# Output turns in 64-row tiles, idle matmuls at the start, and a new order for a fused linear-attention and highway kernel

## The chip, the cores and the metric

The kernel runs on one core of a Trainium2 chip. A core has engines with streams of their own: TensorE (PE, matrix products, with its weight loads shown as PEld), VectorE (DVE), ScalarE (ACT), GpSimd (POOL) and the queues that issue transfers (mainly SyncE, SP). They wait for one another through semaphores. Operands lie in on-chip memory of 128 partitions (SBUF); results of TensorE go to PSUM[...]. The metric is device time of one execution in microseconds (us), lower being better.

## What is computed

Linear attention with a decay per head, in blocks of 64 positions, and behind it a highway layer over all tokens:

```python
# q, k, v: (4, 8, 768, 64); lam: (8,)
for b in range(nb):                          # blocks of 64
    intra = einsum('bhic,bhjc->bhij', qb, kb) * Dmask      # lam^(i-j), lower triangle
    intra = einsum('bhij,bhjd->bhid', intra, vb)
    inter = einsum('bhid,bhde->bhie', qb * lam_pow, kv_state)
    out[block] = intra + inter
    kv_state = lam_block * kv_state + einsum('bhsd,bhse->bhde', kb_dec, vb)

x = out as (3072, 512)                       # tokens x heads*dim
H = maximum(x @ w_h, 0)
T = sigmoid(x @ w_t + b_t)
return T * H + (1 - T) * x                   # float32
```

The kernel works in steps of 256 tokens: 12 steps, three for each of the 4 batch entries. Powers of lam are put into q and v when they are scaled, so that the mask is a plain triangle. The highway result is formed as x + T (H - x).

## The kernel before

Nothing is left to a scheduler: a long string, PLAN, lists operations in order, and each engine runs its own in that order. A token such as `TQ.3.2=0` names the operation, its step and part, and after `=` the PSUM banks; `@ACT` names an engine. What the tokens stand for:

- `Lk/Lq/Lv`: loads of half a step (256 KB, rows of 512 bytes). `W`: half of one weight matrix (512 KB). `CK/CQ/CV`: cast or scaling to bf16. `WC`: cast of weights.
- `TQ/TK`: transposes of q and k on TensorE; `EQ/EK`: their copies out of PSUM.
- `S`, `U`, `SS`: scores and state updates; `KE`: copy of the state; `M`: mask; `I`, `A`: the parts of the attention output from the state and from within the block; `D`: copy of it to bf16, as xT (features x tokens).
- `F.n.u.w`: two 128-feature rows of a product of the highway layer, w=0 for H and w=1 for T; `H`: relu and subtraction; `G`: sigmoid; `X`: th = T (H - x).
- `R`: the output turn, from features x tokens back to tokens x features; `E`: its copy to SBUF; `ST`: its store. `Z`: idle matmuls (the plan before has none).

```python
def trans(x, n, p, bk):                       # TQ, TK: 128x128 tiles
    ...
            T.transpose(t[:, i, j, :], get(x + "b", n)[:, j, h:h + 2, :], id128)

def score(n, e, hp, j, b):                    # 64x64 tiles of the array, 128 columns moved
    T.matmul(get("s", n, e, hp // 2)[half(b), hp % 2, j, :], lhsT=get("kT", n)[half(e), hp, j, half(b)],
             rhs=get("qT", n)[half(e), hp, :, half(b)], start=True, stop=True)

def intra(n, u):                              # A: 16 matmuls in 64x64 tiles
    for hp in (2 * u, 2 * u + 1):
        for j in range(J):
            for b in range(2):
                for e in range(2):
                    T.matmul(get("o", n, b)[half(e), hp, :], lhsT=get("vs", n)[half(b), 2 * hp + e, j, :],
                             rhs=get("m", n, e, u)[half(b), hp % 2, j, :], ...)

def block(i, u, w, bk):                       # F: 8 matmuls of 256 columns, 128x128 tiles
    g, z = group(i)
    t = bank(("ht"[w], g, u), bk[0], [128, 2, z * C])
    for r in range(2):
        for kc in range(KC):
            T.matmul(t[:, r, :], lhsT=w_b[w][:, kc, (2 * u + r) * 128:(2 * u + r + 1) * 128],
                     rhs=get("xT", *g)[:, kc, :], start=(kc == 0), stop=(kc == KC - 1))

def turn(n, b, p, bk):                        # R: 8 matmuls of 128 columns for 128 tokens, one bank
    ...
    for a, j in enumerate(js):
        for i, x in enumerate((get("xT", *g), get("th", g))):
            T.matmul(t[:, a * 128:(a + 1) * 128], lhsT=x[:, j, r * C:(r + 1) * C], rhs=id128,
                     start=(a == 0 and i == 0), stop=(i == 1), skip_group_check=True)

def store(n, b, p):                           # ST: 256 KB for 128 tokens
    i = (2 * n + b) * C
    nc.sync.dma_start(out=out[i:i + C, cs], in_=get("o_sb", n, b, p))

def load_w(w, g):                             # W: 256 columns, rows of 1 KB
    cs = slice(256 * g, 256 * g + 256)
    nc.sync.dma_start(out=w_f[w][:, :, cs], in_=(moe_w_h, moe_w_t)[w][:, cs].rearrange("(kc p) m -> p kc m", p=128))
```

A turn is a product with the identity that adds x and th in PSUM as it transposes them: per step two calls (b = 0, 1) of 8 matmuls each. The last step is split in groups of 128 tokens (and its second 128 tokens' output in two halves), to shorten the end.

Of the kernel before, what the change touches and what calls it, by code (L numbers as in the profile page):

```python
# [17 lines left out]
Lq.0.0 Lq.0.1 Lq.1.0 Lk.0.1 Lv.0.1 Lk.0.0 Lv.0.0 Lk.1.0 CQ.0.1@POOL Lq.1.1 Lv.1.1 CQ.0.0@POOL CK.0.1@ACT Lk.1.1  # L18
TQ.0.0=0 TQ.0.1=1 Lv.1.0 TK.0.1=2 EK.0.1@DVE CK.0.0@POOL Lq.2.1 CV.0.1@DVE TK.0.0=3 EQ.0.1@DVE CV.0.0@POOL Lk.2.0
EQ.0.0@DVE S.0.1=45 EK.0.0@DVE Lq.2.0 U.0.0 S.0.0=62 B=1 KE.0.0@DVE CQ.1.2@POOL W.0.1 M.0.1.0 U.0.1 M.0.0.1 Lk.2.1  # L20
M.0.0.0 CK.1.2@POOL TQ.1.2=0 KE.0.1@DVE I.0=32 W.0.0 EQ.1.2@ACT CV.1.2@POOL TK.1.2=4 M.0.1.1 Lv.2.0 EK.1.2@DVE A.0.1
A.0.0 D.0.1@ACT SS.1.1=60 Lv.2.1 CQ.2.2@POOL KE.1.0@ACT M.1.1.1 W.1.1 D.0.0@ACT M.1.1.0 SS.1.0=54 WC.0.1.0@ACT I.1=20
M.1.0.1 WC.0.1.1@POOL Lk.3.1 TQ.2.2=3 M.1.0.0 CK.2.2@POOL F.0.1.0=6 EQ.2.2@ACT W.1.0 BC A.1.0 WC.0.0.0@DVE
WC.0.0.1@POOL Lk.3.0 A.1.1 TK.2.2=4 D.1.1@ACT D.1.0@DVE F.0.0.0=5 EK.2.2@DVE Lq.3.1 F.1.1.0=1 CV.2.2@POOL KE.1.1@DVE
Lq.3.0 H.0.1 F.1.0.0=3 Lv.3.0 H.1.1 WC.1.1.0@ACT SS.2.0=02 WC.1.1.1@POOL H.0.0 Lv.3.1 SS.2.1=46 M.2.0.0 F.0.1.1=1
Lq.4.1 M.2.1.0 F.1.1.1=5 WC.1.0.1@ACT WC.1.0.0@POOL Lq.4.0 KE.2.0@DVE G.0.1@ACT F.0.0.1=0 M.2.1.1 CK.3.2@POOL Lv.4.1
G.1.1@ACT X.0.1@DVE F.1.0.1=4 Lk.4.0 G.0.0@ACT M.2.0.1 I.2=61 CQ.3.2@POOL Lk.4.1 X.1.1@DVE G.1.0@ACT A.2.0 A.2.1
X.0.0@DVE Lv.4.0 TK.3.2=2 D.2.1@ACT H.1.0 R.0.1.2=5 EK.3.2@ACT Lk.5.1 CV.3.2@POOL TQ.3.2=0 X.1.0@DVE R.0.0.2=1 Lq.5.0
EQ.3.2@ACT D.2.0@DVE R.1.1.2=3 R.1.0.2=4 Lk.5.0 E.0.1.2@ACT CQ.4.2@POOL SS.3.1=26 F.2.1.0=0 Lv.5.0 KE.3.0@ACT M.3.1.1
E.0.0.2@ACT Lv.5.1 M.3.1.0 SS.3.0=56 E.1.0.2@ACT TQ.4.2=1 CK.4.2@POOL Lq.5.1 M.3.0.1 KE.3.1@ACT F.2.1.1=2 EQ.4.2@ACT  # L30
H.2.1 Lq.6.0 CV.4.2@POOL TK.4.2=4 M.3.0.0 G.2.1@ACT I.3=60 Lq.6.1 F.2.0.0=1 EK.4.2@DVE X.2.1@DVE Lv.6.0 A.3.1
SS.4.1=54 H.2.0 CK.5.2@POOL Lq.7.0 A.3.0 F.2.0.1=2 KE.4.0@DVE D.3.1@ACT Lk.6.0 M.4.1.1 D.3.0@ACT SS.4.0=10 G.2.0@ACT
M.4.1.0 CV.5.2@POOL Lk.6.1 F.3.1.1=6 M.4.0.1 Lq.7.1 F.3.0.1=4 X.2.0@DVE Lv.6.1 KE.4.1@DVE CQ.5.2@POOL I.4=50 G.3.0@ACT
F.3.0.0=2 M.4.0.0 Lk.7.1 E.1.1.2@ACT TK.5.2=1 H.3.0 G.3.1@ACT ST.0.0.2 F.3.1.0=3 CQ.6.2@POOL X.3.0@DVE EK.5.2@ACT
Lk.8.1 TQ.5.2=2 H.3.1 R.2.0.2=4 EQ.5.2@ACT Lq.8.1 X.3.1@DVE R.2.1.2=1 A.4.0 E.2.0.2@DVE CK.6.2@POOL Lv.7.1 E.2.1.2@ACT
A.4.1 SS.5.1=36 D.4.1@DVE SS.5.0=24 Lk.7.0 CQ.7.2@POOL D.4.0@DVE R.3.1.2=1 Lv.7.0 TQ.6.2=0 M.5.1.0 E.3.1.2@ACT
TK.6.2=5 M.5.1.1 EQ.6.2@ACT ST.3.1.2 F.4.0.0=3 CV.6.2@POOL M.5.0.1 Lq.8.0 KE.5.0@ACT F.4.1.0=1 M.5.0.0 R.3.0.2=6
EK.6.2@DVE I.5=04 H.4.0 E.3.0.2@ACT SS.6.1=25 H.4.1 ST.3.0.2 A.5.0 A.5.1 ST.1.0.2 KE.6.0@DVE F.4.1.1=6 Lq.9.0
CK.7.2@POOL D.5.0@DVE Lk.9.0 SS.6.0=31 Lq.9.1 G.4.1@ACT D.5.1@DVE F.4.0.1=0 M.6.0.0 KE.6.1@ACT Lk.9.1 F.5.1.1=4
M.6.1.1 G.4.0@ACT Lk.8.0 CQ.8.2@POOL X.4.1@DVE F.5.0.1=3 G.5.1@ACT Lq.10.1 M.6.1.0 F.5.1.0=5 X.4.0@DVE Lv.8.0  # L40
CV.7.2@POOL TK.7.2=6 M.6.0.1 Lv.8.1 TQ.7.2=2 EK.7.2@DVE R.4.1.2=0 Lv.9.0 EQ.7.2@DVE F.5.0.0=1 E.4.1.2@ACT H.5.1
Lk.11.0 G.5.0@ACT I.6=62 A.6.0 H.5.0 SS.7.1=05 CK.9.2@POOL ST.0.1.2 A.6.1 X.5.0@DVE TQ.8.2=1 D.6.1@ACT Lv.9.1
X.5.1@DVE CK.8.2@POOL R.4.0.2=3 D.6.0@ACT TK.9.2=2 KE.7.0@DVE ST.2.1.2 R.5.0.2=4 CQ.9.2@POOL Lq.10.0 M.7.1.0
EK.9.2@ACT F.6.1.0=6 Lq.11.0 E.4.0.2@DVE E.5.0.2@ACT TK.8.2=0 M.7.1.1 EQ.8.2@ACT SS.7.0=23 CV.8.2@POOL H.6.1 ST.1.1.2
TQ.9.2=4 Lk.11.1 EK.8.2@ACT M.7.0.1 F.6.1.1=5 EQ.9.2@DVE I.7=16 Lq.11.1 G.6.1@ACT M.7.0.0 F.6.0.0=3 Lv.10.0
CV.9.2@POOL KE.7.1@ACT X.6.1@DVE SS.8.0=04 Lv.11.1 H.6.0 A.7.1 A.7.0 SS.8.1=25 Lk.10.0 D.7.0@DVE R.5.1.2=3
CQ.10.2@POOL D.7.1@DVE F.6.0.1=1 ST.5.0.2 M.8.0.0 F.7.1.0=6 Lk.10.1 G.6.0@ACT M.8.0.1 CK.11.2@POOL TQ.10.2=0 Lv.11.0
M.8.1.1 KE.8.0@ACT F.7.1.1=4 X.6.0@DVE EQ.10.2@ACT ST.2.0.2 CQ.11.2@POOL F.7.0.0=5 Lv.10.1 M.8.1.0 E.5.1.2@ACT H.7.1
R.6.0.2=1 G.7.1@ACT ST.4.0.2 H.7.0 I.8=02 ST.5.1.2 E.6.0.2@ACT A.8.1 X.7.1@DVE SS.9.1=36 A.8.0 F.7.0.1=5 KE.9.0@ACT
M.9.1.0 M.9.1.1 SS.9.0=14 G.7.0@ACT D.8.0@DVE TK.11.2=3 CK.10.2@POOL D.8.1@DVE KE.9.1@ACT TQ.11.2=6 R.6.1.2=0  # L50
EK.11.2@ACT X.7.0@DVE TK.10.2=2 M.9.0.0 CV.10.2@POOL F.8.1.0=5 E.6.1.2@ACT EK.10.2@DVE EQ.11.2@ACT ST.6.1.2 F.8.0.0=3
M.9.0.1 ST.6.0.2 ST.4.1.2 H.8.1 R.7.1.2=1 CV.11.2@POOL I.9=02 H.8.0 SS.10.1=64 E.7.1.2@ACT A.9.1 A.9.0 KE.10.0@ACT
M.10.1.1 SS.11.0=53 D.9.1@ACT SS.10.0=14 M.11.0.0 D.9.0@ACT F.8.1.1=2 M.10.0.0 R.7.0.2=5 M.10.0.1 I.10=01 M.10.1.0
E.7.0.2@ACT F.9.1.0=4 KE.10.1@DVE ST.7.0.2 A.10.0 ST.7.1.2 M.11.0.1 A.10.1 SS.11.1=56 D.10.1@ACT F.8.0.1=3 KE.11.0@DVE
G.8.1@ACT F.9.1.1=1 D.10.0@ACT X.8.1@DVE G.8.0@ACT F.9.0.1=0 H.9.1 G.9.1@ACT X.8.0@DVE F.10.1.0=2 M.11.1.0 G.9.0@ACT
F.10.0.0=4 M.11.1.1 R.8.0.2=3 X.9.1@DVE I.11=56 E.8.0.2@ACT A.11.0 A.11.1 ST.8.0.2 R.8.1.2=1 D.11.1@DVE F.10.1.1=3
E.8.1.2@ACT H.10.0 D.11.0@ACT F.9.0.0=6 H.10.1 G.10.1@ACT F.10.0.1=1 H.9.0 F.12.0.0=4 X.9.0@DVE G.10.0@ACT F.12.0.1=5
R.9.0.2=2 X.10.0@DVE F.11.1.1=6 E.9.0.2@ACT H.12.0 F.11.0.1=0 G.12.0@ACT X.10.1@DVE ST.9.0.2 F.11.1.0=1 ST.8.1.2
R.9.1.2=2 G.11.1@ACT X.12.0@DVE F.11.0.0=4 H.11.1 E.9.1.2@ACT R.10.1.2=3 H.11.0 G.11.0@ACT ST.9.1.2 R.10.0.2=5
X.11.1@DVE F.12.1.1=1 E.10.1.2@ACT X.11.0@DVE F.12.1.0=2 E.10.0.2@DVE ST.10.1.2 G.12.1@ACT R.11.1.0=4 R.11.0.2=6  # L60
H.12.1 ST.10.0.2 E.11.1.0@ACT X.12.1@DVE ST.11.1.0 E.11.0.2@ACT R.11.1.1=0 ST.11.0.2 E.11.1.1@DVE ST.11.1.1
"""

BUFS = dict(kf=5, qf=5, vf=5, kb=3, qb=2, vs=3, kT=2, qT=3, m=8, xT2=3, xT1=2, th2=2, th1=2, hm2=3, hm1=2, tb2=2, tb1=2, ss=4, o=10, oh=2)
# [3 lines left out]
def kernel(  # L68
# [13 lines left out]
    C = 128  # L82
# [30 lines left out]
    make_identity(nc, id128)  # L113
    tk_i = singles.tile([128, NST, J], I32)
# [10 lines left out]
    V.tensor_copy(id_f, id128[0:KC, 0:KC])  # L125
    ln_bc = singles.tile([128, H], F32)
# [8 lines left out]
    A.preload_act_table(AF.Sigmoid)  # L135
# [14 lines left out]
    def new(key, shape, dtype=BF16, tag=None):  # L150
        if key not in made:
            tag = tag or key[0]
            made[key] = sb.tile(shape, dtype, tag=tag, name=tag, bufs=BUFS[tag])
        return made[key]
# [15 lines left out]
    def load(x, n, p):  # L170
        b, c = divmod(n, NST)
        hs = heads(p)
        nc.sync.dma_start(out=new((x + "f", n), [128, H, J * D], F32)[:, hs],  # L173
                          in_=SRC[x][b, hs, c * 2 * C:(c + 1) * 2 * C, :].rearrange("h (p j) d -> p h (j d)", j=J))

    def load_w(w, g):
        cs = slice(256 * g, 256 * g + 256)
        nc.sync.dma_start(out=w_f[w][:, :, cs], in_=(moe_w_h, moe_w_t)[w][:, cs].rearrange("(kc p) m -> p kc m", p=128))

    def cast_w(w, g, i, eng):  # L180
        ks, cs = slice(2 * i, 2 * i + 2), slice(256 * g, 256 * g + 256)
        copy(eng, w_b[w][:, ks, cs], w_f[w][:, ks, cs])
# [161 lines left out]
    def spin(r, bk, idle=[0]):  # L344
        idle[0] += 1
        t = bank(("spin", idle[0]), bk[0], [128, 128])
        for _ in range(r):
            T.matmul(t, lhsT=id128, rhs=id128, start=True, stop=True)

    DO = {  # L350
        "Lk": lambda a, e, bk: load("k", *a), "Lq": lambda a, e, bk: load("q", *a), "Lv": lambda a, e, bk: load("v", *a),
# [8 lines left out]
        "X": lambda a, e, bk: gate(*a, e), "R": lambda a, e, bk: turn(*a, bk), "E": lambda a, e, bk: evac_o(*a, e),  # L360
# [38 lines left out]
```

## Time and profile before

| | before |
|---|---|
| time, median of 3 | 112.09 us (112.01 to 112.38) |
| span of the profiled execution | 109.5 us |
| PE / PEld busy | 95.4 / 84.8 us |
| DVE / ACT / POOL busy | 84.0 / 66.3 / 60.8 us |
| read / written | 20.98 / 6.29 MB |
| packets of the load and store queue, share of 16 engines | 86.0% |

Busy time of PE is a sum over overlapping, pipelined matmuls, so the start of one matmul to the start of the next tells more than its duration. In the groups by line, the columns are: line, engine, operation, output<-inputs, shapes and count, then busy us and mean ns of one, then the idle time ahead of it and what ended it. In the chain of work in order of time, a row has its start, its length, and the engine, output tile and line, with the number of instructions merged. `bx` is the output turn's PSUM tile, `bh`/`bt` those of the highway products, `bqtr`/`bktr` of the transposes, `bs` of scores, `bo` of the attention output, `kv` the state.

### The profile page before, as it was taken

The numbers are of one execution on the slowest core, as the hardware profiler recorded it, in microseconds if no ns is written. First come the engines' busy times: TensorE is split into PE (matmuls) and PEld (weight loads), VectorE is DVE, ScalarE is ACT, GpSimd is POOL, SyncE is SP. The second block draws the span as 40 slices with busy tenths as digits, with TensorE's granted clock in tenths as the row PEclk, the third lists the DMA queues.
The fourth block names the chain that finished last, engine by engine and source line by source line (L and its number), as shares of the span: only waits on it lengthen the run. The fifth ranks groups of instructions, "written<-read, shape, count | busy, mean of one in ns | idle before, by whom it ended". The sixth has DMA issues, their size and how long they took to land.

```text
span 109.5 us, 4558 instructions
## 1 busy us (share of the span) xinstructions
PE 95.4 (87%) x1969; PEld 84.8 (77%) x1969; DVE 84.0 (77%) x144; ACT 66.3 (61%) x120; POOL 60.8 (55%) x51
## 2 busy tenths in 40 slices
PE   0007887999999999999999999999999999999960
PEld 0005776878889888999888998889898888999950
DVE  0204794739996699799999899899999968867870
ACT  3581034453599867595528279709686639666970
POOL 6073797748489966969737679699319300000000
PEclk9999999999999999999999999999999999999998
DMA  0999999999999999999999999999955331020584
GB/s 9 268 294 291 290 292 328 321 322 317 282 270 299 299 291 297 291 293 301 315 355 313 291 297 314 360 340 310 343 193 195 111 128 70 0 96 6 192 301 178
DMA packets 43899, 27.55 MB, mean 252 GB/s; under 512 B 1764, under 2 KB 40936, under 8 KB 43880
## 3 DMA queue, kind: packets, MB, share of 16 engines
q1 hardware_dynamic: 43728, 27.27, 86.0%
q8 instruction: 15, 0.25, 1.0%
q14 instruction: 4, 0.03, 0.1%
q10 hardware_dynamic: 152, 0.01, 0.1%
HBM read 20.98 MB, written 6.29 MB: 249 GB/s over the span
## 4 chain that ended last, share of the span: by engine, by line
PE 80%; SPq 5%; DMA 5%; DVE 2%; POOL 2%; ACT 2%; issue 1%; DVEq 0%
PE bt L301 20%; PE bh L301 19%; PE bx L328 9%; PE bs L217 8%; PE bo L282 6%; PE bqtr L205 6%; SPq L173 5%; PE bktr L205 5%; DMA qf<-in_q_dram 5%; PE bo L272 5%; PE kv L222 2%; POOL qb L191 2%; DVE o L105 1%; ACT ss L103 1%; ACT o L103 1%
## 5 line engine op out<-in xcount | busy, mean ns | idle before, releaser
L301 PEld LDWEIGHTS <-w_b 128*128 128x128 bf16 x416 | 37.3, 99 | 4.9 <-issue 0.2
L256 DVE TENSOR_TENSOR m<-bs,tri 128x512 bf16<-128x512 f32 x48 | 31.0, 679 | 4.1 <-PE bs L217 3.9
L315 ACT ACTIVATE bt<-bt,bt_col 128x256 f32<-128x256 f32 (+1 forms) x52 | 22.0, 431 | 8.5 <-PE bt L301 5.6
L191 POOL TENSOR_TENSOR qb<-qf,pow_q 128x1024 bf16<-128x1024 f32 (+1 forms) x13 | 23.0, 1772 | 7.0 <-ACT pow_v L134 3.6
L301 PE MATMUL bh<-xT,w_b 128*128 128x256 bf16 (+1 forms) x208 | 25.1, 269 | 0.0
L191 POOL TENSOR_TENSOR vs<-vf,pow_v 128x1024 bf16<-128x1024 f32 (+1 forms) x12 | 22.0, 1835 | 5.5 <-DMA vf<-in_v_dram 5.5
L301 PE MATMUL bt<-xT,w_b 128*128 128x256 bf16 (+1 forms) x208 | 24.0, 265 | 0.0
L319 DVE TENSOR_TENSOR th<-bt,hm 128x512 bf16<-128x512 f32 (+1 forms) x26 | 16.6, 644 | 2.0 <-ACT bt L315 1.2
L105 POOL CAST kb<-kf 128x1024 bf16<-128x1024 f32 (+1 forms) x12 | 12.0, 1003 | 9.7 <-DMA kf<-in_k_dram 6.9
L306 DVE SCALAR_TENSOR_TENSOR hm<-bh,xT 128x512 bf16<-128x512 f32 (+1 forms) x26 | 16.2, 640 | 1.3 <-PE bh L301 1.3
L103 ACT ACTIVATE o<-bx 128x512 f32<-128x512 f32 x20 | 11.8, 597 | 8.8 <-PE bx L328 8.7
L205 PE MATMUL bqtr<-id,qb 128*128 128x128 bf16 x96 | 8.6, 242 | 8.8 <-POOL qb L191 8.8
L217 PE MATMUL bs<-qT,kT 64*64 64x128 bf16 x384 | 15.4, 233 | 0.3 <-DVE qT L105 0.3
L103 ACT ACTIVATE qT<-bqtr 128x1024 bf16<-128x1024 bf16 x9 | 9.2, 1026 | 8.8 <-PE bqtr L205 8.8
L217 PEld LDWEIGHTS <-kT 64*64 64x64 bf16 x384 | 12.1, 115 | 3.1 <-issue 2.3
L205 PEld LDWEIGHTS <-qb 128*128 128x128 bf16 x96 | 6.8, 109 | 9.3 <-POOL qb L191 9.0
L328 PE MATMUL bx<-id,th 128*128 128x128 bf16 x96 | 12.9, 219 | 0.3 <-DVE th L319 0.3
L103 ACT ACTIVATE xT<-bo 128x512 bf16<-128x512 f32 x13 | 9.3, 745 | 6.1 <-PE bo L282 5.9
L328 PE MATMUL bx<-id,xT 128*128 128x128 bf16 x96 | 12.9, 219 | 0.0
L222 PE MATMUL kv<-vs,kb 64*64 64x64 bf16 x320 | 10.0, 205 | 0.9 <-ACT ss L103 0.7
L328 PEld LDWEIGHTS <-th 128*128 128x128 bf16 x96 | 9.4, 98 | 0.5 <-DVE th L319 0.5
L328 PEld LDWEIGHTS <-xT 128*128 128x128 bf16 x96 | 9.3, 98 | 0.3
(43 smaller groups left out, 103.2 us busy)
## 6 DMA issues: line engine op xcount, KB each, us to landing
qf<-in_q_dram SPq DMA_DIRECT2D x24, 256.0 KB, 5.2
kf<-in_k_dram SPq DMA_DIRECT2D x24, 256.0 KB, 5.5
vf<-in_v_dram SPq DMA_DIRECT2D x24, 256.0 KB, 5.4
out_dram<-o SPq DMA_DIRECT2D x23, 256.0 KB, 3.7
w_f<-in_moe_w_h_dram SPq DMA_DIRECT2D x2, 512.0 KB, 6.9
w_f<-in_moe_w_t_dram SPq DMA_DIRECT2D x2, 512.0 KB, 7.6
out_dram<-oh SPq DMA_DIRECT2D x2, 128.0 KB, 1.9
lam_bc<-in_lam_dram ACTq DMA_DIRECT2D x1, 4.0 KB, 3.5
```

What stands on the lines that cost most here:

```text
L103: A.activation(dst, src, AF.Copy)
L105: ENG[eng].tensor_copy(dst, src)
L191: ENG[eng].tensor_tensor(dst, in0=get(src, n)[:, heads(p)].rearrange("p h (j d) -> p h j d", j=J), in1=pw[:, n % NST, heads(p), :, None].t ...
L205: T.transpose(t[:, i, j, :], get(x + "b", n)[:, j, h:h + 2, :], id128)
L217: T.matmul(get("s", n, e, hp // 2)[half(b), hp % 2, j, :], lhsT=get("kT", n)[half(e), hp, j, half(b)], rhs=get("qT", n)[half(e), hp, :, ha ...
L222: T.matmul(kv[half(e), hp, half(e)], lhsT=get("kb", n)[half(b), j, 2 * hp + e, :], rhs=get("vs", n)[half(b), 2 * hp + e, j, :], start=firs ...
L256: V.tensor_tensor(new(("m", n, e, u), [128, 2, J, C]), in0=get("s", n, e, u), in1=tri[:, None].to_broadcast([128, 2, J, C]), op=ALU.mult)
L301: T.matmul(t[:, r, :], lhsT=w_b[w][:, kc, (2 * u + r) * 128:(2 * u + r + 1) * 128], rhs=get("xT", *g)[:, kc, :], start=(kc == 0), stop=(kc ...
L306: V.scalar_tensor_tensor(new(("hm", g, u), [128, 2, z * C], tag=f"hm{z}"), in0=get("h", g, u), scalar=0.0, in1=get("xT", *g)[:, 2 * u:2 * ...
L315: A.activation(dst[:, r, :], src[:, r, :], AF.Sigmoid, bias=bt_col[:, 2 * u + r:2 * u + r + 1])
L319: ENG[eng].tensor_tensor(new(("th", g), [128, NP, z * C], tag=f"th{z}")[:, 2 * u:2 * u + 2, :], in0=get("tt", g, u), in1=get("hm", g, u), ...
L328: T.matmul(t[:, a * 128:(a + 1) * 128], lhsT=x[:, j, r * C:(r + 1) * C], rhs=id128, start=(a == 0 and i == 0), stop=(i == 1), skip_group_c ...
```

## The change

It has five parts. The output turns of steps 0 to 10 are made of 64-row tiles of the array: each of the matmuls is split by the two halves of its input rows, and the halves write to two banks, so that two can be in the array at a time. A step's output then goes out with one store of 512 KB rather than two of 256 KB. Weights are loaded in rows of 2 KB (all 512 columns of 256 rows) rather than of 1 KB; a block F, which takes 128 columns over all 512 rows, then needs both halves of its weight matrix. Idle matmuls on a zero tile (512 columns each, 45 in all in seven places) stand in the plan of the first two steps, to keep TensorE busy while data come in. And the whole order, with banks and engines of the copies, was searched anew, with the fetches of PE's instructions reckoned in. The table of functions for logarithm and exponential is also loaded once, and the one for the sigmoid later, at a place in the plan (`PT`).

```diff
-BUFS = dict(..., qT=3, ..., o=10, oh=2)
+BUFS = dict(..., qT=2, ..., xT4=2, th4=2, ..., o=5, oh=2, oq=1)
+    blank = singles.tile([128, 512], BF16)
+    V.memset(blank, 0.0)
+    A.preload_act_table_set("natural_log_exp_and_others")
     A.activation(ln_bc, lam_bc, AF.Ln)
     ...
-    A.preload_act_table(AF.Sigmoid)
     def load_w(w, g):
-        cs = slice(256 * g, 256 * g + 256)
-        nc.sync.dma_start(out=w_f[w][:, :, cs], in_=(moe_w_h, moe_w_t)[w][:, cs].rearrange("(kc p) m -> p kc m", p=128))
+        nc.sync.dma_start(out=w_f[w][:, 2 * g:2 * g + 2],
+                          in_=(moe_w_h, moe_w_t)[w][256 * g:256 * g + 256].rearrange("(kc p) m -> p kc m", p=128))
     def cast_w(w, g, i, eng):
-        ks, cs = slice(2 * i, 2 * i + 2), slice(256 * g, 256 * g + 256)
-        copy(eng, w_b[w][:, ks, cs], w_f[w][:, ks, cs])
+        copy(eng, w_b[w][:, 2 * g + i], w_f[w][:, 2 * g + i])
+    def turns(n, bk):
+        for r, i in enumerate(bk):
+            bank(("x", n, r), i, [C, 2, KC, 64])
+        for b in range(2):
+            for j in range(KC):
+                for i, x in enumerate((get("xT", n), get("th", (n,)))):
+                    for r in range(2):
+                        T.matmul(get("x", n, r)[:, b, j, :], lhsT=x[half(r), j, b * C:(b + 1) * C], rhs=id128[half(r), half(r)],
+                                 start=(b == 0 and j == 0 and i == 0), stop=(i == 1), skip_group_check=True)
+    def evac_r(n, r, eng):
+        o = new(("o_sb", n), [C, 2, KC, 128], F32, tag="o")
+        copy(eng, o[:, :, :, half(r)], get("x", n, r))
+    def store_r(n):
+        i = 2 * n * C
+        nc.sync.dma_start(out=out[i:i + 2 * C].rearrange("(b p) f -> p b f", p=C), in_=get("o_sb", n).rearrange("p b j f -> p b (j f)"))
     def spin(r, bk, idle=[0]):
-        t = bank(("spin", idle[0]), bk[0], [128, 128])
+        t = bank(("spin", idle[0]), bk[0], [128, 512])
         for _ in range(r):
-            T.matmul(t, lhsT=id128, rhs=id128, start=True, stop=True)
+            T.matmul(t, lhsT=id128, rhs=blank, start=True, stop=True)
 PLAN, its head (all other rows are new too):
-Lq.0.0 Lq.0.1 Lq.1.0 Lk.0.1 Lv.0.1 Lk.0.0 Lv.0.0 Lk.1.0 CQ.0.1@POOL Lq.1.1 Lv.1.1 CQ.0.0@POOL CK.0.1@ACT Lk.1.1
+Lk.0.0 Lv.0.1 Lv.0.0 Lq.0.0 Lk.0.1 Lq.0.1 Lv.1.1 CK.0.0@POOL Lq.1.0 Z.12=0 TK.0.0=0 Lq.1.1 CV.0.0@DVE Lk.1.0
+CQ.0.0@POOL EK.0.0@DVE Lv.1.0 CV.0.1@DVE CK.0.1@ACT Lk.1.1 Z.11=1 TQ.0.0=1 B=2 EQ.0.0@ACT CQ.0.1@POOL W.0.1 W.0.0
+Z.6=0 TQ.0.1=3 TK.0.1=4 EQ.0.1@DVE U.0.0 EK.0.1@ACT W.1.1 S.0.0=56 KE.0.0@DVE S.0.1=01 CQ.1.2@POOL W.1.0 M.0.0.1 Z.1=3
```

and, from the middle, one of the places where a turn stands (before, and after):

```
Lk.8.1 TQ.5.2=2 H.3.1 R.2.0.2=4 EQ.5.2@ACT Lq.8.1 X.3.1@DVE R.2.1.2=1 A.4.0 E.2.0.2@DVE CK.6.2@POOL Lv.7.1 E.2.1.2@ACT

KE.4.1@ACT I.4=14 H.3.1 G.3.1@ACT R.2=25 Lk.8.1 X.3.0@DVE A.4.0 E.2.1@ACT X.3.1@DVE A.4.1 Lk.7.1 SS.5.0=30 E.2.0@ACT
```

## The prediction

> **What bounds the kernel now.** I read the utilisation table by slice first, then the busy time by stretch, the chain that ended last, and the single stages of TensorE.
>
> The busy tenths in 40 slices of 2.74 us:
>
> ```profile
> PE   0007887999999999999999999999999999999960
> PEclk9999999999999999999999999999999999999998
> DMA  0999999999999999999999999999955331020584
> ```
>
> TensorE is full from the 8th slice to the 38th. The DMA engines are full too, up to the 29th slice, and half idle after. So two resources are close to the bound, and stretches tell which one sets the end:
>
> ```profile
> 14.40:24.60 10.20, 9.46 (x181) 8.26 (x182) 5.89 (x11) 4.82 (x7) 7.23 (x7) 1.00 1.15 318
> 24.60:45.00 20.40, 20.40 (x424) 17.72 (x422) 18.51 (x31) 14.09 (x26) 15.93 (x12) 1.00 1.09 293
> 65.00:82.20 17.20, 17.20 (x384) 15.44 (x382) 16.27 (x28) 12.64 (x23) 11.96 (x9) 1.00 1.00 309
> 82.20:105.60 23.40, 23.40 (x465) 21.25 (x462) 19.12 (x34) 16.70 (x37) 3.76 (x2) 1.00 0.30 110
> ```
>
> (Columns: stretch, its length, busy PE, PEld, DVE, ACT, POOL with counts, granted clock, DMA share, GB/s.) From 24.6 to 105.6 us TensorE has no idle time; from 82.2 us on it runs 23.4 us more with DMA at 0.30. TensorE holds the end, DMA is saturated before and is the next limit. The chain says the same: 80% PE, its head a load and its end the last gates and stores.
>
> The chain in order of time shows what each stage costs:
>
> ```profile
> 14.38 1.03 PE bqtr L205 x8
> 21.31 0.85 PE bqtr L205 x8
> 22.16 1.47 PE bh L301 x8
> 47.79 0.45 PE bqtr L205 x8
> 48.23 0.89 PE bx L328 x16
> 49.13 0.57 PE bo L282 x32
> 55.67 0.98 PE bt L301 x8
> 59.94 0.87 PE bh L301 x8
> ```
>
> Three things are in it. Eight transposes take 0.85 to 1.03 us up to 22 us and 0.45 us later, although the granted clock column says 1.00 all along: TensorE runs at half rate until about 23 us, and the column does not tell it. The output turn of one step (16 matmuls of 128 columns, line 328) takes 0.89 us, 55.7 ns each. The 32 matmuls of line 282, in 64x64 tiles, move 128 columns each as well and take 0.57 us with the changes of shape about them: four tiles run beside each other. Their own work is 32 / 4 x 55.7 = 0.445 us, so 0.125 us are the change back, and a block ahead of such a stage takes 0.98 instead of 0.87 us, 0.11 more. A visit to the small tiles costs about 0.24 us on top of its work.
>
> [...] The kernel before has tiles of 128x128 and 64x64 alone, so that no run shows a 64x128 weight load.
>
> **The change, part by part.**
>
> *Turns.* Before, a step has 16 matmuls (2 blocks x 4 column groups x xT and th) of 128 moved columns: 16 x 55.7 = 0.89 us. After, each is split by its 64 input rows: 32 matmuls of 64 columns, the two of a pair on different row halves and banks. If a pair runs together, 16 x 64 columns at 55.7/128 ns = 0.445 us. Steps 0 to 10 are changed: 11 x 0.445 = 4.9 us less. It lies wholly on the path. Against it stand changes of tile shape. Counted in the two plans from the first block of step 0's gate on, with the pair of step 1's A stages, there are 18 visits to small tiles before and 18 after: nearly every R stands next to an A, S or SS. Within the visits there are 11 new changes between 64x64 and 64x128. A full one costs half of 0.24 us; I choose 0.06 us, half of that, as both have 64 rows: 0.7 us. Net 4.2 us less.
>
> *Start.* Idle matmuls on a zero tile (45 of 512 columns) fill the waits. They are to bring the clock up before step 1. Loads are DMA-bound at the start: GpSimd's first waits for data end at 9.70 us for the 6th load and 12.42 us for the 9th, so a load of 256 KB lands each 0.9 us, the first at 5.2. After, the 9th load is Lq.1.1 (12.4); its scaling takes 1.9 us, so TQ.1 starts at 14.3. The 12th is Lk.1.1 (15.1), ScalarE's cast takes 1.0, and TK.1 is free at 16.1; idle matmuls Z.8 (8 x 4 x 55.7 = 1.8 us) hold it until 16.6. Then TK.1 0.45, kT's copy on VectorE 0.7, SS.1.1 0.67, Z.4 0.9, SS.1.0 0.67, I.1 0.45: F.0.0.0 starts near 20.4 us. Its weights are loads 13 and 14, landed by about 18.3, cast by 19. Before, F.0.0.0 starts at 24.6 with TQ.2, TK.2 (0.9), A.1 (0.67) and one block (0.87) already done, which is worth 22.2. Gain: 1.8 us. Z.12 and Z.11 lie in time when there is no data.
>
> *One store per step.* As many copies out of PSUM as before (2 a step), the same bytes; 11 issues less on the queue that also issues loads, each of 0.33 to 1.6 us, but beside PE. The last step keeps its three small stores, so the end after the last matmul stays: 109.5 - 105.6 = 3.9 us. Nothing counted.
>
> *Weights in 2 KB rows.* 2 MB of 21 MB loaded; before, they came in rows of 1 KB, in the slices at 317 to 328 GB/s of the GB/s row, against some 290 beside. A few tenths of a us at most, in a saturated queue. Nothing counted.
>
> *Order and engines.* ScalarE takes more copies (KE 15 instead of 10, D 16 instead of 13), VectorE fewer; by mean durations of 0.6 and 0.7 us some 7 us move. VectorE is at 18.5 of 20.4 us in the stretch from 24.6: this makes room that a faster PE needs. Only one function table is loaded for Ln and Exp, 1.28 us less ahead of pow_q, while scaling waits for its load anyway.
>
> *What the shorter time runs into.* Loads stay at the DMA's rate. Before, the last value loads were awaited by GpSimd at 82.2 us. After, the loads of step 10's values come ahead of step 11's, four transfers earlier, at about 79; scaled at 80.9; SS.10.1 could be reached by TensorE at about 79. Each step's scaling is ready between 0.5 and 4 us ahead of its transposes in a count of this kind. I expect small waits there, and some for instruction fetches (442 more PE instructions, 3939 to 4381): 1.0 us in all, chosen, not derived.
>
> Sum: 112.1 - 4.2 - 1.8 + 1.0 = 107.1 us.
>
> **Rivals.**
> 1. *The weight load binds the turn.* Each pair loads two weights of 128 columns for 64 moved columns. The weight-load record for line 328 is 98 ns, and it hides behind 55.7 ns of start-to-start only because loads run ahead. If a load can't go at below about 28 ns, or the two of a pair go one after the other, a turn stays at 0.89 us or above. Then: 112.1 - 1.8 + 0.7 + 1.0 = 112.0. For it: no 64x128 tile in the trace. Against: 32 weight loads and 32 matmuls of line 282 go in about 0.45 us, 14 ns a pair of instructions, so that issue is no limit.
> 2. *DMA becomes the bound.* Its share is 1.00 or more from 14 to 82 us. If loads don't come earlier than before, the end lies where CV.10 or CV.11 let it: SS.10.1 at about 81 to 82 and from there 19.8 us of TensorE work and 3.9 of tail: 105 to 106 of span. Time is 112.1 where span is 109.5, 2.6 more: 108 to 109 of time. For it: the saturated slices. Against: 8 us of slack between the end of loads and what PE had still to do.
> 3. *The idle matmuls are in the way*, or the clock falls back: they stand in order ahead of real work. If warm-up misses its window, the start gains nothing: 109.
>
> **Range and chances.** The turn's share decides. With pairs complete and no cost of shape changes among 64-row tiles, and no new waits: 105.4. With rival 2 on top of a working turn: 108 to 109. With rival 1: 112. I put 0.8 on the turn being clearly faster. Predicted 107.1 us, 8 in 10 from 104.6 to 111.0; faster by over 2% (below 109.85) 0.80, within 2% 0.15, slower 0.05.
>
> **What would show it.** In the changed profile the turn's 32 matmuls should start within 0.45 to 0.5 us, with pairs at nearly one time; eight transposes of step 1 should take 0.45 us; blocks should begin near 20.4 us; PE should have no idle time from there; GpSimd's waits for DMA should grow somewhat. I am wrong if the turn takes 0.8 us or more, if VectorE or ScalarE ends the waits of PE, or if PE shows gaps on GpSimd's scaling after 60 us.

## The result, and the profile after

| | before, same chip | changed kernel |
|---|---|---|
| time, median | 112.23 us (112.01 to 112.82) | 109.9 us (108.59 to 112.5) |
| ratio, 95% interval | | 0.968 [0.963, 0.973] |

The changed kernel is faster by about 3%. Two of its four executions took 111.03 and 112.5 us and two 108.59 and 108.76, the ratio is taken from the shorter ones, and the profiled one was of the longer (span 109.3 us). So the profile shown here and compared below is that of `after_again`, the same kernel unaltered, with a span of 107.4 us against 109.5 before.

First the page of after_again, busy tenths in 40 slices of 2.69 us:

```profile
PE   4986999999999999999989899999999999999950
PEclk9999999999999999999999999999999999999998
DMA  1799999999999999999999999799999454108264
```

TensorE is now busy from the first slice, with idle matmuls, and two slices in the middle, at 53.7 to 56.4 and 59.1 to 61.8 us, no longer read 9. DMA is as full as before.

The busy times of after_again by stretch (stretch, length, PE, PEld, DVE, ACT, POOL with counts, granted clock, DMA share, GB/s):

```profile
14.40:22.00 7.60, 7.08 (x135) 4.21 (x134) 6.14 (x11) 4.35 (x7) 1.28 (x3) 1.00 1.10 357
22.00:45.00 23.00, 22.82 (x518) 19.38 (x516) 19.79 (x32) 17.04 (x30) 18.04 (x12) 1.00 1.06 285
45.00:65.00 20.00, 19.27 (x463) 17.08 (x461) 17.37 (x29) 15.35 (x26) 13.97 (x10) 1.00 1.12 293
65.00:83.00 18.00, 18.00 (x484) 16.04 (x486) 15.87 (x27) 14.16 (x24) 13.47 (x9) 1.00 0.99 300
83.00:102.90 19.90, 19.90 (x495) 17.93 (x484) 17.22 (x32) 16.23 (x35) 1.90 (x1) 1.00 0.37 135
```

PE lacks 0.2 us of 23.0 in the second stretch and 0.7 us of 20.0 in the third; before, it lacked nothing from 24.6 to 105.6 us. The next engine, VectorE, is busy for 86 to 88% of the last four stretches; the DMA queues are full up to 83 us, as before.

The chain of after_again in order of time, its first part (start, length, engine, tile, line, instructions merged):

```profile
15.15 0.55 PE bqtr L204 x8
15.71 1.74 PE bspin L366 x8
...
17.49 0.61 PE bktr L204 x8
18.10 0.35 PE bo L281 x16
18.44 0.77 PE bspin L366 x3
...
19.98 0.98 PE bspin L366 x4
...
21.65 0.55 PE bo L271 x8
22.20 1.75 PE bh L300 x16
...
33.80 0.57 PE bx L347 x32
```

Eight transposes of step 1 take 0.55 us on the chain, not 1.03: the clock was up early (its record begins at 4.37 us). A whole turn, 32 matmuls of line 347, takes 0.57 us on the chain, where 16 took 0.89. But the idle matmuls (`bspin`) stand in the chain three times, 3.5 us in all, and the first block starts at 22.0 us.

The turn itself, from TensorE's timeline of after_again:

```profile
81.93 0.20 PE L347 MATMUL bx<-id,xT 64*128 64x64 bf16 x2
81.97 0.19 PE L347 MATMUL bx<-id,th 64*128 64x64 bf16 x2
82.00 0.19 PE L347 MATMUL bx<-id,xT 64*128 64x64 bf16 x2
82.03 0.19 PE L347 MATMUL bx<-id,th 64*128 64x64 bf16 x2
```

Each row is a pair on two row halves (x2). The two of a pair start 3 to 4 ns apart, and a pair starts every 30 ns (29.8 in the mean over the 16 pairs of a turn).

### The profile page after: what moved, and what is told of

Its sections match the earlier page's. It is cut to its first block, busy times and chain, and to the rows that moved or that the text cites. A ratio compares the mean times of both kernels' runs of the same rounds, so it can differ in the third digit from the quotient of the medians.

```text
span 109.3 us, 4968 instructions
## 1 busy us (share of the span) xinstructions
PE 99.4 (91%) x2188; PEld 80.6 (74%) x2190; DVE 82.7 (76%) x140; ACT 71.9 (66%) x129; POOL 55.7 (51%) x46
## 4 chain that ended last, share of the span: by engine, by line
PE 61%; DMA 11%; DVE 6%; POOL 5%; ACT 5%; issue 4%; SPq 4%; POOLq 0%; DVEq 0%
PE bt L300 15%; PE bh L300 13%; DMA qf<-in_q_dram 11%; PE bs L216 7%; PE bo L281 5%; PE bx L347 5%; PE bspin L366 4%; PE bqtr L204 4%; DVE m L255 3%; SPq L173 3%; PE bktr L204 3%; POOL qb L190 3%; PE bo L271 3%; ACT qT L101 2%; POOL vs L190 2%
## 5 line engine op out<-in xcount | busy, mean ns | idle before, releaser
L190 POOL TENSOR_TENSOR qb<-qf,pow_q 128x1024 bf16<-128x1024 f32 (+1 forms) x13 | 23.6, 1813 | 11.2 <-DMA qf<-in_q_dram 10.6
L190 POOL TENSOR_TENSOR vs<-vf,pow_v 128x1024 bf16<-128x1024 f32 x10 | 19.0, 1904 | 5.0 <-DMA vf<-in_v_dram 4.6
L101 ACT ACTIVATE xT<-bo 128x512 bf16<-128x512 f32 x16 | 11.5, 749 | 4.6 <-PE bo L281 4.6
L103 POOL CAST kb<-kf 128x1024 bf16<-128x1024 f32 (+1 forms) x10 | 10.0, 995 | 8.1 <-DMA kf<-in_k_dram 6.8
L101 ACT ACTIVATE ss<-kv 128x512 bf16<-128x512 f32 x15 | 8.9, 595 | 7.3 <-PE bs L216 6.1
L366 PE MATMUL bspin<-blank,id 128*128 128x512 bf16 x43 | 11.8, 416 | 1.6 <-POOL id masks.py:199 1.4
L101 ACT ACTIVATE o<-bx 128x512 f32<-128x512 f32 x19 | 10.4, 596 | 1.4 <-PE bx L347 1.3
L101 ACT ACTIVATE qT<-bqtr 128x1024 bf16<-128x1024 bf16 (+1 forms) x10 | 9.8, 980 | 1.8 <-PE bqtr L204 1.8
L281 PE MATMUL bo<-m,vs 64*64 64x128 bf16 x384 | 9.4, 219 | 0.7 <-DVE m L255 0.4
L366 PEld LDWEIGHTS <-id 128*128 128x128 bf16 x45 | 4.3, 105 | 6.4 <-issue 1.7
L281 PEld LDWEIGHTS <-vs 64*64 64x64 bf16 x384 | 6.6, 106 | 2.4 <-issue 1.5
```

What stands on the lines that cost most here:

```text
L101: A.activation(dst, src, AF.Copy)
L103: ENG[eng].tensor_copy(dst, src)
L190: ENG[eng].tensor_tensor(dst, in0=get(src, n)[:, heads(p)].rearrange("p h (j d) -> p h j d", j=J), in1=pw[:, n % NST, heads(p), :, None].t ...
L366: T.matmul(t, lhsT=id128, rhs=blank, start=True, stop=True)
```

## The experiments

Edits are against the changed kernel unless it says otherwise. "Stream" below is the time from the first matmul of the first block (F.0.0.0) to the first of the last turn (R.11.1.0), read from the timeline; from there to the end it is 4.2 to 4.8 us in all of them.

### The same kernel again

No edit.

> The changed kernel once more, unaltered, for a second profile. Instruction-fetch theory: TensorE's program comes in blocks of 256 instructions; a block is usable about 1.4 us after its transfer has ended, the transfer starts 0.3 to 3.9 us after the block before was entered, and where that is longer than the block itself TensorE stands still at the block's edge. So the gaps of the first profile (0.41 to 1.47 us, at four edges, 2.8 us in all) sit at edges again, though not all the same ones, and their sum is smaller if the time is nearer 108.7. Rival (waits for GpSimd's scaled data): the gaps sit ahead of transposes and score stages, with GpSimd named as what ended them.

Measured: 109.44 us, ratio 0.974 [0.969, 0.980]; F.0.0.0 at 22.04 us, stream 80.94 us. The gain is there again, and so is the late first block.

### All parts but the turns

```diff
-    for r in range(2):
-        T.matmul(get("x", n, r)[:, b, j, :], lhsT=x[half(r), j, b * C:(b + 1) * C], rhs=id128[half(r), half(r)], ...)
+    T.matmul(get("x", n, b)[:, j, :], lhsT=x[:, j, b * C:(b + 1) * C], rhs=id128, ...)
-        copy(eng, o[:, :, :, half(r)], get("x", n, r))
+        copy(eng, o[:, b], get("x", n, b))
```

> The changed kernel with its turns made of 128-row tiles again (16 matmuls of 128 columns, one bank for each 128 tokens), in the new order, with the new stores and the idle matmuls; 352 instructions of TensorE fewer. If the turn's split is worth what its stage shows (0.89 less 0.54 us, 11 times: 3.9 us, and about 0.24 us where a visit to the small tiles is cut in two, some 3 times), and nothing is given back: 4 to 4.6 us longer than the changed kernel, 113. Fetch theory: the split gives back 1 to 3 us at block edges, which this kernel doesn't pay: only 1 to 3 us longer, 110 to 112, and no gap over 0.15 us at edges.

Measured: 112.05 us, ratio 1.000 [0.997, 1.004]. The turn in TensorE's timeline of turn128:

```profile
82.89 0.22 PE L346 MATMUL bx<-id,xT 128*128 128x128 bf16 x1
82.94 0.22 PE L346 MATMUL bx<-id,th 128*128 128x128 bf16 x1
83.00 0.22 PE L346 MATMUL bx<-id,xT 128*128 128x128 bf16 x1
```

One matmul each 56 ns, 16 of them. Summed over steps 0 to 10, from the first matmul of a turn to what follows it, the stage takes 10.44 us here and 6.18 us in after_again: 4.26 us. The new order, stores, weight rows and idle matmuls together are worth nothing with the old turn. The stream is 83.58 us, so that of the 4.26 us only 2.64 are kept: 1.6 us is given back in the same order of work. Operation by operation, it lies in seven places. The stages A (6.45 to 7.00 us) and TK (4.54 to 5.08) have grown in one operation each, A.5.0 by 0.56 and TK.7.2 by 0.53: 1.09 together. And five operations in 128x128 tiles that stand right ahead of a turn (F.2.1.0, I.4, F.6.1.1, F.8.0.0, F.12.1.0) take 0.10 us more each, 0.50 together (F 42.68 to 43.09, I 4.45 to 4.54). That is what a change of tile shape costs ahead of a turn.

### The turns alone, in the order of before

Edit against the kernel before; `turns`, `evac_r` and `store_r` are those of the change, banks are fitted anew so that two are given to a turn, in all eleven steps:

```diff
-o=10, oh=2)
+o=5, oh=2, oq=1)
 PLAN, one of eleven places:
-R.1.1.2=3 R.1.0.2=4 ... E.1.0.2@ACT ... E.1.1.2@ACT
+R.1=34 E.1.0@ACT E.1.1@ACT
```

> The kernel before with the new turns alone (and the one store they need), at the place of the later of a step's two turns, all else in the old order; the turns mostly stand alone among 128-row stages, so each pays a whole visit of 0.24 us. By the stages: 0.89 - (0.54 + 0.2) = 0.15 us a step, 1.6 us less than before, 110.5. If the turn's gain needs the new order, or moved turns hold buffers too long: same as before or slower, 112 to 114.

Measured: 123.2 us, ratio 1.089 [1.080, 1.098]: far off what was expected. SyncE's waits in before_turns, the longest:

```profile
SPq L313 <- ACT o L60: 29.9, 4, 8.7
```

Stores stand in the same queue as loads and wait for the output's copies (29.9 us, 4 times); in two slices in the middle DMA moves only 55 and 71 GB/s. So the stores were moved in the next run.

### The same with its first stores behind the last load

```diff
-o=5
+o=10
 PLAN: ST.0 to ST.3 stand behind the last load
```

> before_turns again, with the stores of steps 0 to 3 moved behind the last load, so that no load stands behind a store that waits for its data, and ten output buffers of a step. If the loss of before_turns came from loads stuck behind stores: the holes in the DMA row are gone and the time is 110 to 112.5, a turn worth 0.15 us a step. If it came from the later turns' hold on banks and buffers: still over 114.

Measured: 123.52 us, ratio 1.090 [1.080, 1.100]. The holes in DMA are gone (no slice below 222 GB/s from the 2nd to the 28th), the time is the same, so they were not its cause. What remains are waits of TensorE: from 24 us on they sum to 10.4 us, where the kernel before has 0.3. Two of them in before_turns_late:

```profile
PE bx L304 <- DVE m L213: 2.3, 1, 2.3
PE bx L304 <- ACT o L60: 1.2, 1, 1.2
```

A turn (`bx`) reads neither the masked scores `m` nor an output `o`. What it waits for here can only be that these copies empty a PSUM bank that the turn is to write. Waits of this kind, for a copy whose result the waiting operation does not read, are 7.1 of the 10.4 us. So the loss lies mostly in banks, of which a turn now takes two at once. What the pair shows is that in this old order, with the turns put in this way, the faster turn is a loss.

### No idle matmuls

```diff
-Z.12=0  -Z.11=1  -Z.6=0  -Z.1=3  -Z.8=1  -Z.3=5  -Z.4=0    (in the plan)
```

> The changed kernel without its 45 idle matmuls (90 instructions). If they bring the clock up in time for steps 0 and 1, this kernel starts its first block of the highway 1 to 2 us later and ends 1 to 2 us later, 110 to 111. If the start is bound by loads, and the idle matmuls are only in the way: the first block starts at the same time or earlier, and the end is at 108 to 109. By the fetch theory the edges move by 90 rows, so the gaps stand at other stages of the plan.

Measured: 110.38 us, ratio 0.984 [0.975, 0.993]. F.0.0.0 is at 21.84 us, but cold: the block takes 1.42 us there, 0.87 in after_again, and the first clock record begins at 22.94 us; F.0.1.0 follows at 23.26 (22.91 with them) and TQ.2.2 at 28.30 (27.95). All 45 idle matmuls are worth 0.35 us there, and the rest of the stream is alike: the last turn starts at 103.32 us, against 102.97.

### Without the three groups on the chain

```diff
-Z.8=1  -Z.3=5  -Z.4=0    (in the plan; 30 fewer instructions, Z.12, Z.11, Z.6, Z.1 stay)
```

> The changed kernel with the idle matmuls of the first step alone (Z.12, Z.11, Z.6, Z.1: 30); Z.8, Z.3 and Z.4, which stand ahead of real work of step 1, are gone. Theory: the clock is up by 4.4 us and needs no more of them, while these three hold TK.1, SS.1.1 and SS.1.0 back. Then the first block F.0.0.0 starts when the last cast of its weights is done, 20.2 to 20.8 us instead of 22.0, and with step 2's data ready at 26.2 the end is 1 to 1.5 us earlier: 107.5 to 108.3. Rival: loads bind the stages behind it, so that the time won is lost again in waits for data: 108.7 to 109.4. Second rival: TensorE falls back to half rate between steps: eight transposes take 0.85 us again, first block at 21.8, 109.5.

Measured: 110.58 us, ratio 0.977 [0.969, 0.985]: no better than the changed kernel. The start did gain: F.0.0.0 at 20.35 us, TQ.2.2 at 26.43 instead of 27.95. It was lost on the way: TQ.11.2 stands at 86.14 against 85.28, and the stream is 83.62 us long, 2.68 more than in after_again. TensorE's timeline of few_idle shows two of the places (idle time ahead of a row in square brackets):

```profile
33.27 0.40 PE L161 MATMUL bqtr<-id,qb 128*128 128x128 bf16 x4
34.39 0.40 PE L161 MATMUL bqtr<-id,qb 128*128 128x128 bf16 x4 [0.72 <-issue]
...
70.11 0.26 PE L178 MATMUL kv<-vs,kb 64*64 64x64 bf16 x6
71.45 0.24 PE L173 MATMUL bs<-qT,kT 64*64 64x128 bf16 x1 [1.08 <-issue]
```

Both gaps lie inside one operation, of which nothing new has to be waited for: four of eight transposes have gone, and the other four read the same tiles. `issue` says that the profile shows nothing that TensorE waited for. Three gaps of this kind take 2.75 us, 1.66 more than the two of after_again; the other 1.0 us lies in small waits, the largest 0.3 us for step 2's kT.

### What such a gap is: the blocks of PE's instructions

The pages give queue 8 as `instruction`. Before, then after_again:

```profile
q8 instruction: 15, 0.25, 1.0%
```

```profile
q8 instruction: 17, 0.28, 1.1%
```

15 packets of 16 KB before and 17 after, for 3938 and 4380 recorded rows of PE and PEld: some 260 rows a packet, and the gaps below, on a grid of 256 rows, give it as 256 instructions. I took the start and end of each packet from the trace and laid them beside TensorE's rows. The gaps of turn64x64 (an experiment below) stand ahead of rows 1215, 1471, 1983, 2495 and 3519, each 256 n - 65, and those of the other kernels on the same grid (two rows later where two rows more are recorded). At each such edge, where TensorE enters a new block, the transfer of the block behind it starts: from about then to 4 us later while loads run. A transfer mostly lasts 0.9 to 1.2 us (at most 2.5). No block is entered sooner than 1.27 us after the end of its own transfer, and at each of the 19 gaps below its first row comes 1.27 to 1.62 us after it. So when TensorE has used up its block before the next one is there, it stands still exactly at the edge. Edges between 28 and 91 us; the delay is from the first row of a block to the end of the transfer that starts there (the kernel before has no gap that marks its edges, so that its delays are good to about 0.1 us):

```
kernel        delay mean / max    gaps at edges over 0.225 us, from row to row
before        2.4 / 3.0           none
turn128       2.2 / 3.5           none
after         3.3 / 4.8           0.49  0.44  0.41  1.47    (profile of the first set)
after_again   3.0 / 4.2           0.58  0.58
two_stores    3.0 / 4.0           0.47  0.31  0.25
no_idle       2.6 / 3.7           0.34  0.85
few_idle      3.3 / 4.7           0.93  0.54  1.28
turn64x64     2.9 / 5.0           0.99  1.64  2.52  1.77  3.29
light_loads   1.5 / 3.2           none
```

Why the delay is shorter in before and turn128, beside DMA queues as full, no run shows.

What the next block costs is not always hidden behind the one before it: from 34 to 85 us a block lasts 4.6 to 5.7 us where nothing holds it up (light_loads), and a delay of up to 4.2 us (after_again) and 1.3 to 1.6 us from the transfer's end to the first row can come to more than that.

The two edges of after_again are what A.5.0 and TK.7.2 lost above. The first in its timeline:

```profile
53.62 0.28 PE L281 MATMUL bo<-m,vs 64*64 64x128 bf16 x4
54.26 0.31 PE L281 MATMUL bo<-m,vs 64*64 64x128 bf16 x8 [0.36 <-issue]
```

At the second the profile names another releaser, VectorE's `th`:

```profile
59.05 0.50 PE L204 MATMUL bktr<-id,kb 128*128 128x128 bf16 x6
59.91 0.38 PE L271 MATMUL bo<-qT,ss 128*128 128x128 bf16 x4 [0.36 <-DVE th L318]
```

The timeline of light_loads (below; its lines are shifted by three) tells that this is not so:

```profile
58.45 0.68 DVE L321 TENSOR_TENSOR th<-bt,hm 128x512 bf16<-128x512 f32 x1
...
58.90 0.39 PE L274 MATMUL bo<-qT,ss 128*128 128x128 bf16 x4
```

There the same matmul starts 0.23 us ahead of the end of the same `th`. So it doesn't depend on it; `th` merely ended last before a gap that the edge made.

### More instructions for the same work

Each turn matmul in two of 64x64: 704 more PE instructions (352 matmuls and their weight loads), with the columns of weights halved and the array's work unchanged.

```diff
-                    for r in range(2):
-                        T.matmul(get("x", n, r)[:, b, j, :], lhsT=x[half(r), j, b * C:(b + 1) * C], ...)
+                    for s in range(2):
+                        for r in range(2):
+                            T.matmul(get("x", n, r)[half(s), b, j, :], lhsT=x[half(r), j, b * C + 64 * s:b * C + 64 * s + 64], ...)
```

> The changed kernel with each of the turn's 64x128 matmuls cut into two of 64x64: 64 matmuls of 64 columns on four tiles, the same work for the array, 704 instructions of TensorE more (2.75 blocks of 256). Array theory (instructions cost nothing as long as the array is shared): the turn stays at 0.5 to 0.6 us, the time at 108.7 to 109.4, or a little less as shapes don't change within a visit. Fetch theory: the dense blocks would be used up in about 4 us and can't come faster than one in 4.6 to 6.3 us while loads run; 14 or so blocks lose 0.5 to 2 us each: 114 to 122, with gaps at block edges, every 256 instructions.

Measured: 120.36 us, ratio 1.067 [1.058, 1.076]; span 118.6 us, 11.2 more than after_again. TensorE's timeline of turn64x64:

```profile
52.26 0.27 PE L216 MATMUL bs<-qT,kT 64*64 64x128 bf16 x3
54.83 0.21 PE L216 MATMUL bs<-qT,kT 64*64 64x128 bf16 x1 [2.30 <-issue]
...
83.81 0.23 PE L216 MATMUL bs<-qT,kT 64*64 64x128 bf16 x2
87.12 0.24 PE L216 MATMUL bs<-qT,kT 64*64 64x128 bf16 x1 [3.08 <-issue]
```

Gaps at eight edges (the five above and 0.42, 0.23, 0.27 us later) sum to 11.1 us, 10.0 more than the two of after_again, nearly all in work that has nothing to do with turns. Another 1.5 us is a fall of the clock after the gap of 2.52 us (its record reads 0.5 from 55.00 to 58.41 us, and TQ.6.2, TK.6.2 and F.4.1.0 take 3.3 us instead of 1.8). The turn's own stage takes 0.53 to 0.78 us outside R.1, into which an edge falls, against 0.48 to 0.57. It is the count of instructions in a stretch that costs.

### The loads taken away

Steps 3 to 11 use the q, k and v that steps 0 to 2 loaded, so the output isn't the reference's; every computation stays.

```diff
+        if n >= 3:
+            made[(x + "f", n)] = made[(x + "f", n % 3)]
+            return
```

> The changed kernel with q, k and v loaded for steps 0 to 2 alone; later steps use the same data again, so its output is not the reference's. All instructions of TensorE stay. Fetch theory, with DMA queues as the cause of the delay: after 25 us the transfer of a block starts within 0.8 us of the edge before it, is usable some 2.5 us after the edge, and no gap is at an edge; TensorE's stream from F.0.0.0 to the last turn takes 1 to 1.5 us less than in the changed kernel (80.9), about 79.5. If the delay has nothing to do with loads, fetches start 1 to 3.9 us after the edges as before. If loads are what holds the changed kernel back otherwise (GpSimd waiting for them): over 2 us less.

Measured: 108.09 us (one run), span 106.4. The DMA row of its page:

```profile
DMA  0899999994000220000000000880055055008264
```

From the 11th slice on the DMA engines are idle but for instructions and stores. The delay falls to a mean of 1.5 us, no edge has a gap, and the stream is 79.85 us, 1.09 less than in after_again, as was expected with the fetch as the cause. The difference lies in two operations: A.5.0 takes 0.43 us instead of 0.98 and TK.7.2 0.45 instead of 0.97, and every other one from F.0.0.0 on agrees within 0.01 us. So the full DMA queues make the fetches late, and the two gaps are all that they cost TensorE here. Loads were not the bound as data: with two thirds of the loaded bytes gone, no wait for data has gone with them.

### Shorter transfers ahead of the fetch

Each q, k, v load as two of 128 KB instead of one of 256 KB:

```diff
-        nc.sync.dma_start(out=new((x + "f", n), ...)[:, hs], in_=SRC[x][b, hs, ...])
+        for h in range(hs.start, hs.stop, 2):
+            nc.sync.dma_start(out=new((x + "f", n), ...)[:, h:h + 2], in_=SRC[x][b, h:h + 2, ...])
```

> The changed kernel with each load of q, k and v cut into two of 128 KB (144 instead of 72). At most eight loads are under way at a time, as a load waits for the completion of the one eight before it, so that half the bytes stand in the queues. If the bytes that are queued are what delays the fetch of a block of instructions: fetches start 1 us or less after the edge (2.0 on average before, from 25 to 90 us), no gap at edges, 1 us less than the changed kernel, 107.5 to 108.3. If the delay only goes with busy DMA engines, however few loads stand in line: fetches as before, 108.6 to 109.6. If the queue that issues the loads is too slow for twice as many (0.4 to 0.5 us each at best): GpSimd waits longer for data, over 110.

> few_idle with the small loads. If small loads make fetches quick, the 1.5 us won at the start are kept: 106.5 to 107.5, the fastest of all. If not: gaps at edges again, 109 to 110.6, as few_idle.

few_small is the same edit on few_idle. Measured: small_loads 125.73 us (123.41 to 126.44), few_small 124.13 us, ratio 1.107 [1.101, 1.114]. The issues of loads (KB each, median us to landing) in after_again and in small_loads, and GpSimd's longest waits in small_loads:

```profile
kf<-in_k_dram SPq DMA_DIRECT2D x24, 256.0 KB, 5.4
```

```profile
kf<-in_k_dram SPq DMA_DIRECT2D x48, 128.0 KB, 3.3
```

```profile
POOL qb L191 <- DMA qf<-in_q_dram: 14.4, 9, 2.5
POOL kb L103 <- DMA kf<-in_k_dram: 11.1, 6, 3.5
```

Of the loads under way at a time, the trace of `after` shows this: SyncE's transfers carry eight semaphores in turn, each issue ends at least 1.2 us after the landing of the eighth before it, and at most seven are under way at the end of an issue. Here, a load lands 3.3 us after its issue instead of 5.4, but the rate of DMA falls to 190 to 250 GB/s in most slices from about 290, and GpSimd waits for data. TensorE is so much slower that no edge has a gap. The transfers of instruction blocks do start earlier, 1.0 and 0.9 us after the edge in the mean against 1.8 and 2.1 without the edit, as was expected if queued bytes delay them. But the DMA engines are less busy as well (packets of the load queue fill 73 to 75% of the span, 88% in after_again), so these two runs don't tell which of the two it is. That stays open.

### Two stores per step again

```diff
-        nc.sync.dma_start(out=out[i:i + 2 * C]..., in_=get("o_sb", n)...)
+        for b in range(2):
+            nc.sync.dma_start(out=out[i + b * C:i + (b + 1) * C], in_=get("o_sb", n)[:, b]...)
```

> The changed kernel with each 512 KB store issued as two of 256 KB, one behind the other, at the same place. Stores are beside TensorE's stream and the last step's stores are unchanged: 108.6 to 109.6, no difference from the changed kernel. If one store per step is worth something, 0.5 us or more longer, with later loads.

Measured: 108.88 us, ratio 0.974 [0.969, 0.979], the same as the changed kernel within the interval. One store per step shows no gain.

### The earlier start without loads

few_idle and light_loads together (output as in light_loads not the reference's):

> few_idle with q, k and v loaded for steps 0 to 2 alone, as in light_loads (its output is not the reference's). If few_idle's earlier first block (20.35 against 22.04 us) is lost only to late instruction blocks and late data while loads run: the gain comes through here, a span of 104.7 to 105.2, 1.2 to 1.7 us under light_loads' 106.4, no gap at edges from 35 us on. If another engine takes it back (VectorE or ScalarE ahead of the blocks): 106 to 106.5, as light_loads.

Measured: 108.79 us (one run), span 107.1, where less was expected than light_loads. Its TensorE clock row:

```profile
PEclk9999999959999999999999999999999999999998
```

F.0.0.0 starts at 21.56 us, 1.2 later than in few_idle. TensorE waited 1.78 us for ScalarE's copy of the state, which stands behind the cast of a weight half that came 1.0 us later here (19.09 us) than in few_idle (18.06). Then the clock fell: the trace's clock record reads 0.5 from 20.95 to 24.36 us, and the eight matmuls of F.0.0.0 take 1.71 instead of 0.87 us.

The clock records of the fourteen traces show when that happens. Their lengths are whole multiples of 3.41 us (3.41, 10.24, 13.65, 47.79, 102.40), at another offset in each execution. With TensorE's busy time laid over that grid, the clock fell, ahead of the tail, after seven stretches of 3.41 us, which were 18, 33, 39, 42, 42, 46 and 47% busy. It stayed up after all the others, of which the least busy had 51, 52 and 54%. Four of them, from light_few, few_small and, twice, turn64x64 (columns as in the stretches of after_again; the clock fell after the first three and stayed after the fourth):

```profile
17.54:20.95 3.41, 1.34 (x67) 1.13 (x68) 2.83 (x7) 1.75 (x3) 1.22 (x2) 1.00 1.09 352
13.76:17.17 3.41, 1.60 (x34) 1.03 (x28) 3.10 (x5) 0.96 (x2) 1.26 (x1) 1.00 0.96 291
51.59:55.00 3.41, 1.11 (x67) 0.96 (x56) 1.76 (x3) 1.60 (x3) 1.90 (x1) 1.00 1.08 302
82.31:85.72 3.41, 1.73 (x141) 1.57 (x140) 2.42 (x5) 1.23 (x2) 2.15 (x2) 1.00 0.92 321
```

So in these traces a stretch on the grid that was at most 47% busy was followed by a lower clock in the next one, and one of at least 51% was not. With the three groups, in light_loads and after_again, any 3.41 us between 13 and 23 us are at least 89% busy. In few_idle the emptiest are 47% busy, while the two on its grid are 67 and 79%: that its clock stayed up is in part luck. So the three groups guard the clock at the price of 1.5 us. From TQ.2.2 to the last turn light_few and light_loads take 73.94 us both, each operation alike within 0.01 us, but TQ.2.2 came later here (28.85 against 28.02 us), so that whether an early start would survive to the end without loads isn't settled.

## Why the prediction was right, and where not

107.1 us was predicted; 109.9 and 109.44 us were measured, inside the range. The direction was right, for the reason given; the gain was 5.0 us in the sum and 2.9 to 3.6 on the chip (ratio 0.974 of 112.33 and 0.968 of 112.23). Of the signs named in advance, the turn's 32 starts within 0.45 us and eight transposes of step 1 in 0.45 us came true, blocks from 20.4 us on and no idle time after them did not.

- *Turns, 4.2 us.* Right in mechanism, and nearly in size. A pair goes each 30 ns, and the stages take 4.26 us less (turn128 beside after_again). Against that, the five operations ahead of a turn lose 0.50 us, so that 3.8 us are left. The first rival falls: the 64x128 weight load (95 ns in the records) hides behind pairs 30 ns apart. That halves on two banks run together, which had no run behind it, is now seen (3 to 4 ns apart); whether two halves in one bank would, no run tried.
- *Start, 1.8 us.* This is the step that failed. F.0.0.0 was put at 20.4 us; it stands at 22.04, against 22.15 for the same state before (24.59 less 2.44): 0.1 us. On the chip TQ.1 starts at 15.1 (14.3 predicted), TK.1 at 17.5 (16.6), SS.1.1 at 19.4 (17.8), SS.1.0 at 21.0 (19.3). The first 0.8 us is not late data: GpSimd has scaled q by 14.5, but TQ.1 stands behind A.0.1, and that waits for VectorE's mask until 14.7, a step that the count left out. Then k's cast is ready at 16.3 and Z.8 holds TK.1 for 1.2 us more, where the count had 0.5 on the path; the copy of kT ends at 18.8 and Z.3, behind A.0.0, holds SS.1.1 to 19.2, neither of which was in the count. Without Z.8, Z.3 and Z.4 the block does start at 20.35 (few_idle). That idle matmuls bring the clock up was an assumption, which no trace of the kernel before showed; it held: the first clock record of the trace begins at 4.37 us in after_again, at 22.94 in no_idle and at 23.25 before (the nines of a clock row ahead of that stand where there is no record). But it bought only what the idle matmuls cost. The third rival was right about their being in the way.
- *Waits, 1.0 us, chosen.* The size came out (1.09 us), but by luck, as the main cause was another: not scaling behind loads but two edges of instruction blocks. No gap on GpSimd's scaling appears in after_again. Yet few_idle shows that the edges are linked to the start: move the stream by 1.5 us and take out 30 instructions, and they fall on other places, with 2.75 us of gaps.
- *Second rival, DMA as the bound.* In the form stated, late data, it falls: taking away most loads saves 1.0 us of span, all of it at the two edges. The DMA queues cost through TensorE's instructions instead. The rival's own sum was too high as well: it set the time of 112.1 beside the span of another execution; the profiled one of 109.5 took 111.24 us, 1.7 more and not 2.6, so that the rival meant 107 to 108 us.
- *Stores and weight rows, nothing counted.* Right for stores (two_stores). Weight rows were tried only as part of turn128, whose sum is nothing.
- *Copies moved to ScalarE, some 7 us.* Five state copies of 0.6 us and three of 0.75 make 5.2; its busy time grew by 5.5 us.
- *The tail* was counted as unchanged. From the first matmul of the last output piece to the end it is 4.4 us (102.97 to 107.4) against 4.1 before (105.40 to 109.5): 0.3 longer, in turn128 as well.

Beside turn128, whose time is that of the kernel before, the measured terms add up: 112.05 - 4.26 (turns) + 1.09 (the two edges) + 0.50 (ahead of turns) = 109.4 us, against 109.44.

## What to carry to other kernels

Splitting a matmul of 128 moved columns by its input rows, into two tiles that run together, nearly halved its time here (a pair each 30 ns instead of one each 56), but it doubles instructions, and a TensorE stream that uses 256 instructions in about 5 us beside full DMA queues waited for its own program: look for gaps marked `issue` inside an operation, and count rows from one gap to the next. Idle matmuls that warm the clock belong where data aren't there yet; on the chain they cost here what they brought, and taking them out can leave a stretch so empty that the clock drops (39% busy over 3.41 us in light_few). Change one part of such a plan and keep the rest, and the gain may turn into a loss, as the turns alone in the old order did.

## What the runs showed of the hardware that was not expected

- The fetch of PE's instructions has a delay of 2.2 to 3.3 us in the mean from block edge to end of transfer under full DMA, 1.5 us without most loads, and another 1.3 to 1.6 us pass to the first row where TensorE waits for it; 704 more instructions cost 11 us of span.
- The clock fell after stretches of 3.41 us that were 18 to 47% busy, and not after ones of 51% or more. The length of a single wait did not decide it: in light_few the longest wait ahead of the fall was 1.78 us, and in turn64x64 the clock stayed up over a wait of 3.08 us, which lay across two stretches of 51 and 59%.
- 128 KB transfers of 512-byte rows, issued from one queue, moved 190 to 250 GB/s in most slices where 256 KB ones moved about 290.
